# Feature map folded into the query and key weights: six heads per matmul in 120 rows instead of two row tiles of three heads

## The chip, the cores and the metric

The kernel runs on one core of one Trainium2 chip. The metric is the device time of one execution in microseconds (us); lower is better. The time of a kernel is the median of its runs.

## The reference

The kernel computes a linear-attention block with a learned feature map, gated by an MLP. Only block A is touched by the change; what matters of it is:

```
xn   = layernorm(x)                                   # x: 2048 tokens, 640 wide
q, k, v = split(xn @ wqkv)                            # 32 heads of 20 columns each
pq   = einsum("bhsd,hdf->bhsf", q, w_phi)             # one 20x20 matrix per head
pk   = einsum("bhsd,hdf->bhsf", k, w_phi)
phi  = concat(softmax(p), softmax(-p))                # for pq and for pk
o    = phi_q (phi_k^T v) / (phi_q sum(phi_k) + 1e-6)
out  = x + (o @ wo) * silu(gelu(xn @ w1 + b1) @ w2 + b2)
```

Since pq = xn @ (wq of head h @ w_phi of head h), the kernel multiplies the weights with the feature map first and never forms q or k. This product of weights is called the fold here. There are two of them, for keys and for queries, each a 640x640 matrix made from 32 products of 640x20 with 20x20.

## The kernel before, in words

**Stages.** The first stage (to about 259 us of the span) goes over 16 tiles of 128 tokens: each is normalised, transposed on TensorE (`transpose_x`, L293, for the first tiles; the later ones are loaded transposed), and projected (`project`, L307) onto the folded key weights `wk_s`, the value weights `wv_s` and the folded query weights `wq_s`. Feature maps are exponentials per head; `kv_acc` (L378) accumulates phi_k^T v. The second stage is the MLP (L617, L646), the last one the query side and the output projection (L736 to L811). TensorE works in fp32r, with operands split in a high and a low part, in the projections, and in plain fp32 in the fold.

**Where the fold stands.** A fold covers one chunk of 128 input rows (c = 0 to 4) of the key or query weights: `fold(tl, c)` issues its matmuls into one tile `pA` of two PSUM banks, and `fold_w` lets ScalarE copy the result to the high part (L173, fp32r) and VectorE subtract to get the low part (L174). The five key folds come first in the program: folds 0 and 1, the transposes of tile 0, folds 2, 3 and 4, and then the key projection of tile 0. The five query folds stand one by one among the projections of tiles 3 to 6. Tile `pA` has three buffers, which projections, folds and transposes take in turn.

**The operands.** The weights of a fold arrive transposed: in `folds`, partition r and slot i of chunk c hold one column of wq or wk over 128 input rows. Before the change, slot i of six holds heads 3i to 3i+2 of the first 16 heads in partitions 0 to 59, and the same three of the last 16 heads in partitions 64 to 123; slot 5 holds one head of each half, in 20 partitions. `foldb` holds the feature maps of these heads as blocks on a diagonal, 64 columns wide per slot. For each slot two matmuls are issued, one for partitions 0 and up, one for partitions 64 and up, each into its own bank. `_layout`, on the host, only places the inputs in that order.

**What sets the order.** The order on every engine in this part of the program is written out by hand (`manual_schedule`). All loads go through one queue, SP's. It starts with the feature maps (L443), chunk 0 of the key weights (L153), the first tile of x (L131), the other four chunks of the key weights, and two more tiles of x; the five value weights (`raw`, L144), further tiles and the query weights follow. Before the first fold TensorE runs eleven matmuls of a 128x128 tile of ones (L440), which compute nothing that is used.

The rest that the prediction touches: `norm` (L187 to L198 on VectorE, L190 on GpSimd) normalises the next tile; `plain` (L227 on ScalarE, L229 on VectorE) splits a transposed tile; `split_w` (L136, L138) splits the value weights.

Of the kernel before, what the change touches and what calls it, by code (L numbers as in the profile page):

```python
# [8 lines left out]
F32 = mybir.dt.float32  # L9
# [5 lines left out]
S, D, H, DH, F = 2048, 640, 32, 20, 1536  # L15
P = 128
# [4 lines left out]
KC = D // P  # L21
# [24 lines left out]
def hedgehog_gated_mlp_kernel(ctx: ExitStack, tc: tile.TileContext, x, xt_in, wqk, bd, wv, wo, w1, b1, w2, b2, out_t):  # L46
    nc = tc.nc
# [7 lines left out]
    xpool = xstack.enter_context(tc.tile_pool(name="xpool", bufs=1))  # L55
    xpool.tile([P, 16], F32, name="xpad")
    xp = xpool.tile([P, 8, 2, CW], F32R, name="xp")
    foldt = xpool.tile([P, 2 * KC * 6 * P + 6 * 64], F32, tag="D", name="folds")
    folds = foldt[:, :2 * KC * 6 * P].rearrange("p (w c i t) -> p w c i t", w=2, c=KC, i=6)
    foldb = foldt[:, 2 * KC * 6 * P:].rearrange("p (i t) -> p i t", i=6)  # L60
    xds = []
# [21 lines left out]
    def bankA():  # L83
        return pools["A"].tile([P, 2, 512], F32, tag="A", name="pA")
# [73 lines left out]
    def fold(tl, c):  # L158
        ps = bankA()
        for i in range(6):  # L160
            n = 60 if i < 5 else 20
            for hf in range(2):
                r = slice(64 * hf, 64 * hf + n)
                mm = nc.tensor.matmul(ps[:, hf, 60 * i:60 * i + n], tl[r, c, i, :], foldb[r, i, :n],  # L164
                                      start=True, stop=True)
        return ps, mm

    def fold_w(tl, cs, name, dst):
        for c in cs:
            ps, mm = fold(tl, c)  # L170
            sl = slab(F32R, f"{name}{c}")
            s3 = sl[:].rearrange("p s (a b) -> p s a b", a=2)
            nc.scalar.activation(s3[:, 0], ps[:, :, :HALF], AF.Copy)  # L173
            lo = nc.vector.tensor_tensor(s3[:, 1], ps[:, :, :HALF], s3[:, 0].bitcast(F32), op=OP.subtract)  # L174
            dst.append(sl)
        return mm, lo
# [657 lines left out]
    for unit in range(units):  # L834
        h, g = divmod(unit, NG)
# [169 lines left out]
def _layout(A_x, A_wqkv, A_w_phi, A_wo, B_w1, B_b1, B_w2, B_b2):  # L1005
    import numpy as np
    a = {k: np.asarray(v) for k, v in dict(x=A_x, wqkv=A_wqkv, wphi=A_w_phi, wo=A_wo, w1=B_w1, b1=B_b1,
                                           w2=B_w2, b2=B_b2).items()}
    wqk = np.zeros((2, KC, P, FOLD_W), a["wqkv"].dtype)
    bd = np.zeros((P, 6, 64), a["wphi"].dtype)  # L1010
    wo = np.zeros((680, D), a["wo"].dtype)
    for k in range(10):
        wo[64 * k:64 * k + 60] = a["wo"][60 * k:60 * k + 60]
    wo[640:] = a["wo"][600:]
    for h in range(H):
        i, k = divmod(h % 16, 3)
        r = slice(64 * (h // 16) + DH * k, 64 * (h // 16) + DH * (k + 1))
        for w in range(2):
            for c in range(KC):
                wqk[w, c, r, i * P:(i + 1) * P] = a["wqkv"][c * P:(c + 1) * P, w * D + h * DH:w * D + (h + 1) * DH].T  # L1020
        bd[r, i, DH * k:DH * (k + 1)] = a["wphi"][h]
    return [
        ("x", a["x"].reshape(S, D)),
        ("xt", np.ascontiguousarray(a["x"].reshape(S, D).T)),
        ("wqk", wqk),
        ("bd", bd),
        ("wv", np.ascontiguousarray(a["wqkv"][:, 2 * D:])),
        ("wo", wo),
        ("w1", np.ascontiguousarray(a["w1"].reshape(KC, P, NF, P).transpose(2, 1, 0, 3).reshape(NF, P, D))),
        ("b1", np.ascontiguousarray(a["b1"].reshape(NF, P).T)),  # L1030
        ("w2", np.ascontiguousarray(a["w2"])),
        ("b2", np.ascontiguousarray(a["b2"].reshape(KC, P).T)),
    ]
# [18 lines left out]
```

## Time and profile before

| what | value |
|---|---|
| time, median of 3 runs | 693.31 us |
| lowest and highest run | 691.02 and 696.13 us |
| span of the profiled execution | 688.8 us |
| own time of the profiled execution | not shown; the span lies 4.5 us under the median of the runs |
| PE busy | 680.1 us, 99% of the span, 4833 matmul records |
| PEld (weight loads) busy | 592.8 us, 86% |
| VectorE, ScalarE, GpSimd busy | 66%, 36%, 55% |
| mean granted TensorE clock | 0.996 |
| HBM traffic | 125.57 MB, mean 182 GB/s |

The profile shows one execution. PE is TensorE's matmul side and PEld its weight loads; an fp32 matmul of the program leaves two matmul records and two weight loads in the trace, an fp32r matmul one of each. A record's duration holds the pipeline's latency, so the pace of a stream is read from the starts of successive records. A timeline row gives the start, the time from the first start to the last end, the engine, line and operation, the tiles, the shapes (the weights first, then output or moving shape) and the count. Times in rows are us from the span's start.

### The profile page before, as it was taken

To read this page: it belongs to the slowest core of one execution; us is meant where nothing else is said; L and a number is where in the kernel's file an instruction comes from. 1 tells how busy PE (TensorE), PEld (TensorE's weight loads), DVE (VectorE), ACT (ScalarE), POOL (GpSimd) and SP (SyncE) were. 2 spreads that over 40 slices of the span, in tenths; PEclk is the share of its full clock that TensorE was granted. 3 is DMA by queue.
4 is the path that set the end of the run, shared out by engine and by line. 5 is a ranking of instruction groups with operands and counts; after the bars stand their busy time and mean duration, and the time that the engine had idled before them with its cause. 6 is when DMAs were issued, how large, how long until landed. Compare 5 with 4: busy or idle time off the path is not lost.

```text
span 688.8 us, 12182 instructions
## 1 busy us (share of the span) xinstructions
PE 680.1 (99%) x4833; PEld 592.8 (86%) x4833; DVE 453.4 (66%) x730; ACT 251.3 (36%) x398; POOL 376.8 (55%) x336
## 2 busy tenths in 40 slices
PE   8899999999999999999999999999999999999997
PEld 8899999999999998888888888888888887777875
DVE  4688556887667546667978774677977655774232
ACT  3331322332332227343353346632232353425430
POOL 1354344948587455946878853636356640783221
PEclk9999999999999999999999999999999999999999
DMA  9830052824172144328697697276364391886633
GB/s 327 288 104 2 3 149 79 245 68 160 35 212 77 72 145 169 115 69 292 220 328 253 202 429 323 81 272 230 140 218 152 132 391 65 320 292 203 234 92 107
DMA packets 73967, 125.57 MB, mean 182 GB/s; under 512 B 5694, under 2 KB 42686, under 8 KB 73014
## 3 DMA queue, kind: packets, MB, share of 16 engines
q1 hardware_dynamic: 71606, 114.31, 48.8%
q10 hardware_dynamic: 2304, 10.49, 4.3%
q8 instruction: 38, 0.62, 0.4%
q14 instruction: 19, 0.16, 0.1%
HBM read 79.68 MB, written 45.10 MB: 181 GB/s over the span
## 4 chain that ended last, share of the span: by engine, by line
PE 96%; DMA 1%; DVE 1%; issue 1%; POOL 1%; ACT 0%; SPq 0%; POOLq 0%; DVEq 0%
PE pA L307 30%; PE pB L646 24%; PE pB L617 21%; PE pB L805 11%; PE pB L747 3%; PE pA L164 2%; PE pB L736 2%; PE kv L378 2%; DMA folds<-in_wqk_dram 1%; PE pA L293 1%; PE pB L754 1%; PE pB L591 0%; POOL e L328 0%; POOL wv L138 0%; ACT e L333 0%
## 5 line engine op out<-in xcount | busy, mean ns | idle before, releaser
L646 PE MATMUL pB<-hs,w2s 128*128 128x512 f32 x720 | 167.1, 390 | 0.0
L646 PEld LDWEIGHTS pB<-hs,w2s 128*128 128x128 f32 x720 | 134.7, 188 | 29.3 <-PE pB L747 0.8
L617 PE MATMUL pB<-xp,w1s 128*128 128x512 f32 x324 | 81.3, 389 | 0.0
L617 PE MATMUL pB<-xd,w1s 128*128 128x512 f32 x324 | 79.3, 389 | 0.0
L333 ACT ACTIVATE e<-e 128x1280 f32<-128x1280 f32 x32 | 40.7, 1271 | 90.0 <-POOL e L328 90.0
L805 PE MATMUL pB<-oT,wo 128*128 128x512 f32 x300 | 72.9, 395 | 0.0
L655 DVE TENSOR_TENSOR y<-pB,y 128x512 f32<-128x512 f32 x100 | 63.8, 680 | 12.3 <-PE pB L646 12.1
L617 PEld LDWEIGHTS pB<-xd,w1s 128*128 128x128 f32 x324 | 60.8, 188 | 12.6
L617 PEld LDWEIGHTS pB<-xp,w1s 128*128 128x128 f32 x324 | 60.8, 188 | 12.6
L805 PEld LDWEIGHTS pB<-oT,wo 128*128 128x128 f32 x300 | 55.4, 188 | 14.8 <-ACT ph L739 1.2
L346 POOL TENSOR_TENSOR e<-e,rc 128x1280 f32<-128x1280 f32 x16 | 39.0, 2438 | 49.1 <-DVE rc L366 48.8
L346 POOL TENSOR_TENSOR eq<-eq,rc 128x1280 f32<-128x1280 f32 x16 | 37.9, 2370 | 50.2 <-DVE rc L705 50.2
L328 POOL TENSOR_TENSOR e<-nr,e 128x640 f32<-128x640 f32 x32 | 45.5, 1422 | 34.6 <-DVE nr L327 31.7
L307 PE MATMUL pA<-wv,xp 128*128 128x320 f32 x384 | 61.1, 312 | 0.8 <-DVE nr L327 0.4
L307 PE MATMUL pA<-wk,xp 128*128 128x320 f32 x384 | 61.5, 316 | 0.0
L622 ACT ACTIVATE pB<-pB,b1t 128x512 f32<-128x512 f32 x48 | 31.8, 662 | 76.2 <-PE pB L617 26.7
L307 PE MATMUL pA<-wq,xp 128*128 128x320 f32 x384 | 59.0, 309 | 0.0
L307 PEld LDWEIGHTS pA<-wk,xp 128*128 128x128 f32 x384 | 58.3, 193 | 0.2
L307 PEld LDWEIGHTS pA<-wv,xp 128*128 128x128 f32 x384 | 56.9, 188 | 1.7 <-issue 0.7
L307 PEld LDWEIGHTS pA<-wq,xp 128*128 128x128 f32 x384 | 56.9, 188 | 0.1
L692 POOL TENSOR_TENSOR ez<-eq,zrep 128x1280 f32<-128x1280 f32 x16 | 47.3, 2958 | 0.5 <-DMA eq<-e_dram 0.5
L402 POOL TENSOR_TENSOR w1s<-raw,w1s 128x640 fp32r<-128x640 f32 (+1 forms) x18 | 25.7, 1429 | 37.1 <-ACT w1s L401 29.9
(139 smaller groups left out, 1045.2 us busy)
## 6 DMA issues: line engine op xcount, KB each, us to landing
raw<-in_w_dram SPq DMA_DIRECT2D x42, 320.0 KB, 4.4
e_dram<-e ACTq DMA_DIRECT2D x16, 640.0 KB, 4.0
eq<-e_dram SPq DMA_DIRECT2D x16, 640.0 KB, 7.0
phi_dram<-eq SPq DMA_DIRECT2D x16, 640.0 KB, 3.5
phi<-phi_dram SPq DMA_DIRECT2D x16, 640.0 KB, 8.5
xt<-in_x_dram SPq DMA_DIRECT2D x16, 320.0 KB, 4.9
xres<-in_xt_dram SPq DMA_DIRECT2D x20, 256.0 KB, 4.8
out_dram<-xres SPq DMA_DIRECT2D x18, 256.0 KB, 3.0
```

The lines of the kernel that those rows point to most:

```text
L307: nc.tensor.matmul(ps[:, hf, :HALF], stat_x(q, o, k, a), ws[k][:, b, hf * HALF:(hf + 1) * HALF], start=n == 0, stop=n == 3 * KC - 1)
L328: nc.gpsimd.tensor_tensor(e5[:, :, :, 1, :], nr[:, :, :, None].to_broadcast([P, 2, 16, DH]), e5[:, :, :, 0, :], op=OP.subtract)
L333: nc.scalar.activation(ef, ef, AF.Exp)
L346: nc.gpsimd.tensor_tensor(e3, e3, rc[:, :, None].to_broadcast([P, 64, DH]), op=OP.mult)
L402: nc.gpsimd.tensor_tensor(sl[:, 1, :n], src, sl[:, 0, :n].bitcast(F32), op=OP.subtract)
L617: nc.tensor.matmul(bank[ch][:], tl[:, a, off + wo_:off + wo_ + P], mov(blk, b), start=new and n == 0, stop=n == len(mms) - 1, skip_group_c ...
L622: nc.scalar.activation(ps, ps, AF.Gelu_apprx_tanh, bias=b1t[:, f:f + 1])
L646: nc.tensor.matmul(ps[:], ws[i][:, b, d * P:(d + 1) * P], hs[o][i][:, a, :], start=i == n == 0, stop=(i, n) == (GF - 1, 2), skip_group_che ...
L655: nc.vector.tensor_tensor(y, ps[:], y, op=OP.add)
L692: nc.gpsimd.tensor_tensor(zv, ef, zf, op=OP.mult)
L747: nc.tensor.matmul(po[64 * e:64 * e + 64, :256], bdk[:n, 2 * j + e, :], ph[:n, e * 256:(e + 1) * 256], start=True, stop=True)
L805: nc.tensor.matmul(ps[:], w, o, start=n == 0, stop=n == 15)
```

## The change

The six slots of a chunk are filled in another way: slots 0 to 2 hold the first 16 heads (six, six and four of them), slots 3 to 5 the last 16, all from partition 0 on, in 120, 120 and 80 partitions. A fold is then six matmuls of 120 (or 80) rows and 120 (or 80) columns instead of twelve of 60 (or 20). The same columns of the same banks are written. `foldb` becomes 120 columns wide per slot, so its load grows from 384 to 720 values per partition. Nothing else differs: the weights' load has the same size, and all other engines issue the same instructions in the same order. From L164 on, line numbers are lower by one in the changed kernel.

```
-    foldt = xpool.tile([P, 2 * KC * 6 * P + 6 * 64], F32, tag="D", name="folds")
+    foldt = xpool.tile([P, 2 * KC * 6 * P + 6 * 120], F32, tag="D", name="folds")
...
     def fold(tl, c):
         ps = bankA()
         for i in range(6):
-            n = 60 if i < 5 else 20
-            for hf in range(2):
-                r = slice(64 * hf, 64 * hf + n)
-                mm = nc.tensor.matmul(ps[:, hf, 60 * i:60 * i + n], tl[r, c, i, :], foldb[r, i, :n],
-                                      start=True, stop=True)
+            hf, j = divmod(i, 3)
+            n = 120 if j < 2 else 80
+            mm = nc.tensor.matmul(ps[:, hf, 120 * j:120 * j + n], tl[:n, c, i, :], foldb[:n, i, :n],
+                                  start=True, stop=True)
         return ps, mm
...
-    bd = np.zeros((P, 6, 64), a["wphi"].dtype)
+    bd = np.zeros((P, 6, 120), a["wphi"].dtype)
...
-        i, k = divmod(h % 16, 3)
-        r = slice(64 * (h // 16) + DH * k, 64 * (h // 16) + DH * (k + 1))
+        j, k = divmod(h % 16, 6)
+        i, r = 3 * (h // 16) + j, slice(DH * k, DH * (k + 1))
```

The PE queue around a query fold that follows `kv_acc`, in tile 5, before (a row is a run of matmuls: line, operation, output tile and operand, output shape, count):

```order
L378 MATMUL kv<-e,v 32x40 x32
L164 MATMUL pA<-folds 128x60 x10
L164 MATMUL pA<-folds 128x20 x2
L307 MATMUL pA<-wv,b_749 128x320 x12
L307 MATMUL pA<-wv,xp 128x320 x6
```

and the same place in the changed kernel:

```order
L377 MATMUL kv<-e,v 32x40 x32
L163 MATMUL pA<-folds 128x120 x2
L163 MATMUL pA<-folds 128x80
L163 MATMUL pA<-folds 128x120 x2
L163 MATMUL pA<-folds 128x80
L306 MATMUL pA<-wv,b_719 128x320 x12
L306 MATMUL pA<-wv,xp 128x320 x6
```

Twelve matmuls have become six in the same place; the instructions around them stand as before.

The head of SP's queue of loads, before:

```order
L443 DMA folds<-in_bd_dram 128x384
L153 DMA folds<-in_wqk_dram 128x768
L131 DMA xt<-in_x_dram 128x640
L153 DMA folds<-in_wqk_dram 128x768 x4
L131 DMA xt<-in_x_dram 128x640 x2
```

and in the changed kernel:

```order
L442 DMA folds<-in_bd_dram 128x720
L153 DMA folds<-in_wqk_dram 128x768
L131 DMA xt<-in_x_dram 128x640
L153 DMA folds<-in_wqk_dram 128x768 x4
L131 DMA xt<-in_x_dram 128x640 x2
```

The first load is larger; the order is the same.

## The prediction

> **What bounds the kernel now.** First the page's busy shares and its chain that ended last, then TensorE's waits: which engine carries the span, and whether anything holds it up.
>
> ```profile
> PE 96%; DMA 1%; DVE 1%; issue 1%; POOL 1%; ACT 0%; SPq 0%; POOLq 0%; DVEq 0%
> PE pA L307 30%; PE pB L646 24%; PE pB L617 21%; PE pB L805 11%; PE pB L747 3%; PE pA L164 2%; PE pB L736 2%; PE kv L378 2%; DMA folds<-in_wqk_dram 1%; PE pA L293 1%; PE pB L754 1%; PE pB L591 0%; POOL e L328 0%; POOL wv L138 0%; ACT e L333 0%
> PE pA L293 <- DVE xt L198: 1.3, 1, 1.3
> PE pA L440 <- POOL ones L102: 1.2, 1, 1.2
> PE pA L164 <- DMA folds<-in_wqk_dram: 0.5, 1, 0.5
> PE pA L307 <- DVE nr L327: 0.4, 1, 0.4
> PE pA L307 <- POOL wv L138: 0.2, 1, 0.2
> ```
>
> PE carries the chain, and these five are all of its waits, each once and all at the start. So what the fold (L164, 2% of the chain) saves on PE shortens the span, and the most that could be saved is those 2%, some 16 us. The question is the pace of a fold. Here is TensorE's timeline at the start, and the stretch of L440's stream of 128x128 fp32 matmuls with its group's durations (minimum/median/maximum).
>
> ```profile
> 5.49 1.66 PE L164 MATMUL pA<-folds 60*128 60x60 f32 x24
> 7.63 1.66 PE L164 MATMUL pA<-folds 60*128 60x60 f32 x24 [0.48 <-DMA folds<-in_wqk_dram]
> 9.38 0.74 PE L293 MATMUL pA<-ident,xt 128*128 128x128 f32 x5
> 10.05 4.83 PE L164 MATMUL pA<-folds 60*128 60x60 f32 x72
> 14.82 4.44 PE L307 MATMUL pA<-wk,xp 128*128 128x320 f32 x18
> 19.09 0.71 PE L293 MATMUL pA<-ident,xt 128*128 128x128 f32 x5
> 4.83 0.72 PE L440 MATMUL pA<-ones 128*128 128x128 f32 x5
> L440 PE MATMUL pA<-ones x22: 274/421/579, 1.2 to 5.3; 128*128 128x128 f32 x22
> 59.44 1.21 PE L164 MATMUL pA<-folds 60*128 60x60 f32 x17
> ```
>
> The last row is the inside of one query fold. Its 17 records start in nine groups, the odd one and then eight pairs: one row tile of 60 starts together with the other. The eight steps take 1.21 less a last record's 0.272, or 0.94 us: 0.117 us a pair, the first step the longest. In L440 five records take 0.72 us; less the last one's 0.274, four steps of 0.111 us. **So a pair of 60-row records and one full 128x128 record cost the same 0.11 us**: the two tiles already run at once. Three folds in a row take 14.82 - 10.05 = 4.77 us, 1.59 each, for twelve pair steps (1.33 us at 0.111). The 0.26 us beyond them is what a fold loses at its changes of shape, from 128 rows to 60, to 20 and back.
>
> The clock is the second thing in that stretch: the table of stretches, with PE busy, its records, and the granted clock.
>
> ```profile
> 4.00:8.08 4.08, 3.60 (x43) 3.31 (x44) 1.25 (x4) 0.70 (x1) 0.05 (x1) 1.00 0.97 312
> 8.08:11.49 3.41, 3.32 (x49) 2.94 (x47) 2.76 (x4) 1.41 (x2) 0.51 (x1) 1.00 1.03 407
> 11.49:14.90 3.41, 3.41 (x53) 3.19 (x52) 2.21 (x6) 1.41 (x2) 0.28 (x1) 1.00 1.04 410
> 14.90:18.31 3.41, 3.41 (x13) 3.41 (x14) 2.08 (x3) 0.70 (x1) 0.27 (x1) 0.50 1.03 408
> ```
>
> For 3.41 us right behind the key folds the clock is halved, though PE was busy for all 3.41 us before. What was low there is how much the matmuls feed: a fold streams ten pair steps of 60 columns and two of 20, 640 columns in 1.59 us, while L440's pace would bring 128 x 1.59/0.111 = 1830; that is 35%.
>
> **The change, part by part.** *Query folds.* Each becomes 12 records, six of 120 (or 80) columns twice, one after the other. Three of the five stand between projections. The rows of such a place, and of the same projections without a fold:
>
> ```profile
> 36.85 2.00 PE L307 MATMUL pA<-wv,xp 128*128 128x320 f32 x12
> 38.70 4.56 PE L307 MATMUL pA<-wk,xp 128*128 128x320 f32 x30
> 43.19 0.84 PE L378 MATMUL kv<-e,v 128*32 128x40 f32 x64
> 43.96 2.91 PE L307 MATMUL pA<-wv,xp 128*128 128x320 f32 x18
> 46.71 0.71 PE L293 MATMUL pA<-ident,xt 128*128 128x128 f32 x5
> 57.49 2.00 PE L307 MATMUL pA<-wv,xp 128*128 128x320 f32 x12
> 59.43 1.66 PE L164 MATMUL pA<-folds 60*128 60x60 f32 x24
> 61.02 4.66 PE L307 MATMUL pA<-wk,xp 128*128 128x320 f32 x30
> 65.61 0.84 PE L378 MATMUL kv<-e,v 128*32 128x40 f32 x64
> 78.48 1.66 PE L164 MATMUL pA<-folds 60*128 60x60 f32 x24
> 80.07 2.03 PE L307 MATMUL pA<-wv,b 128*128 128x320 f32 x12
> ```
>
> With the fold 61.02 - 57.49 = 3.53 us, without it 38.70 - 36.85 = 1.85: 1.68. The projection behind takes 65.61 - 61.02 = 4.59 against 43.19 - 38.70 = 4.49, so 0.10 more, its first weight load being late. That is 1.78 us a fold. Now 12 x 0.111 = 1.33 in unbroken 128-row work: a gain of 0.45, three times 1.35. The other two follow `kv_acc`, whose own tiling spoils the next load anyway: 80.07 - 78.48 = 1.59 becomes 1.33, twice 0.26. Together **-1.87 us**.
>
> The step of 0.111 us has bounds. The trace holds no 120-row fp32 stream of 120 columns. If columns set the pace, the step shrinks to 0.111 x 120/128 = 0.104 and 0.111 x 80/128 = 0.069: a fold of 1.11, another 0.22 less. If the weight load is no longer hidden, the 0.10 of the late load comes on each record: 0.21. I take 0.111, since 60 columns and 128 have the same step, which speaks for the weight load, 128 columns in both, as what sets it; and L440, one full tile behind the other, is the nearest row.
>
> *The larger first load.* 128 x 336 x 4 bytes = 172 kB at 312 to 410 GB/s is 0.42 to 0.55 us; I take 0.45, as the next loads run near 407. All loads behind it land that much later. Fold 0 is covered: it starts 0.2 us after the last L440 and shows no wait. Fold 1 isn't, its chunk ends its wait now: 7.63 becomes 8.08, and the transposes of tile 0, whose load shifts as well, 9.83 for 9.38.
>
> *Key folds.* The rows of VectorE that the next steps lean on:
>
> ```profile
> 9.15 1.75 DVE L174 TENSOR_TENSOR wk<-pA,wk 128x640 fp32r<-128x640 f32 x2
> 12.49 0.82 DVE L174 TENSOR_TENSOR wk<-pA,wk 128x640 fp32r<-128x640 f32 x1 [0.77 <-ACT wk L173]
> 15.21 0.61 DVE L198 TENSOR_SCALAR xt<-xt,st 128x640 f32<-128x640 f32 x1 [0.67 <-POOL st L190]
> 15.74 1.55 DVE L174 TENSOR_TENSOR wk<-pA,wk 128x640 fp32r<-128x640 f32 x2
> 20.64 0.42 DVE L229 TENSOR_TENSOR b<-pA,b 128x256 fp32r<-128x256 f32 x1 [3.35 <-ACT xp L227]
> ```
>
> Fold 2 takes fold 0's buffer, free halfway through the 9.15 row at 10.0; now 10.5. Three folds of 1.33 end at 14.5 for 14.82: **-0.30 us**, the late load paid. Cover for the rest: fold 3's buffer must be free for tile 1's transposes, and the tile normalised; VectorE does this by 16.5 (half of the 15.74 row) plus 0.45, so 17.0.
>
> *The clock.* A fold now streams 8 x 120 + 4 x 80 = 1280 columns in 1.33 us, 83% of L440's pace. So I expect the halved stretch to go. The first 18 matmuls of the key projection take 19.09 - 14.82 = 4.27 us now, and 46.71 - 43.96 = 2.75 elsewhere at the full clock (likewise with a late first load): **-1.52 us**. By the clock itself, 3.41 x 0.5 = 1.71; I keep the rows. Tile 1's transposes then start at 14.5 + 2.75 = 17.25, just behind the 17.0 of VectorE, and for 19.09. From there a chain over VectorE, GpSimd and ScalarE leads to the value projection at 33; it starts with ScalarE's copy of these transposes and VectorE's L229 (20.64), and moves with them. From 33 on PE is dense, and nothing is seen to wait, so I let the whole shift stand.
>
> The sum is -1.87 - 0.30 - 1.52 = -3.7 us. Against its own execution: a span of 688.8 becomes 685.1. Its own time isn't shown; its span lies 4.5 us under the median of 693.31. With that kept, **689.6 us**.
>
> **What the Trainium skill says.** "TensorE: Matmul & The Clock Gate", section "HAM oscillation — how this bites in real kernels", has it that the clock falls where PE idles for more than about 3.4 us between bursts. The trace differs: PE was busy for all of the 3.41 us before the fall. By that rule the fold's shape would not matter to the clock, which is the first rival below. The same page of the Trainium skill, in the section "The mechanism" of its Part 3, says that weight loads overlap with matmuls in flight only when their row groups differ, as they did between the two row tiles and no longer do. L440's 0.111 us speaks against it; by that rule the second rival would come.
>
> **The rivals.** (1) *The clock falls all the same* (it hangs on something else than columns streamed). For it: I have one fall in one execution, and the stretch 8.08 to 11.49, also thin in columns, was not followed by one. Against: nothing else is special there. Then only -1.87 - 0.30 = -2.2: 691.1 us. (2) *Slower: each weight load waits for the matmul before it*, in the fold's own stream. Before, successive loads went to different row tiles. At 0.21 us a record a fold takes 2.53 us: query folds 3 x (2.53 - 1.78) + 2 x (2.53 - 1.59) = +4.1; fold 1 from 8.08 to 10.6, the transposes to 11.3, three folds to 18.9, +4.1 for 14.82, and the clock's fall stays. 701.5 us. It decides from 0.13 us a record on (2.2 us over 120 records is 0.018 above 0.111). Against it stands L440's pace on full rows. (3) *The later first load thins out the start*: fold 0 ends near 6.9, fold 1 waits to 8.08, and the idle gap brings a fall of the clock from there, 1.7 us on the folds, in place of the one lost: about -3.7 + 1.7, 691.3 us. For it: a wait of 1.1 us instead of 0.48. Against: fold 0 alone streams 1280 columns there instead of 640.
>
> **How the numbers follow.** The forecast 0.60, the first rival 0.23, the third 0.11, the second 0.06. All but one lie within 1% (6.9 us), which is about what a measurement of this kernel can tell from no change. The three runs of before lie 5.1 us apart, so a median can be off by 2 us or more. The range goes from 686.5 (the forecast, less the 2.2 of the column-paced step and some scatter) to 694.0 (rivals 1 and 3 with the scatter of runs); only rival 2 is left out. Faster by over 1% needs the column-paced step and luck in the runs, 0.07; slower by over 1% is rival 2, 0.06; the rest 0.87.
>
> **What would show it.** L164's work becomes 120 records at line 163, with steps of 0.11 us and no gap inside; a query fold between projections adds 1.33 us. No stretch of half clock behind the key folds, and tile 1's transposes at about 17.3 us. Fold 1 begins near 8.1. Steps of 0.2 us would prove the sum wrong, and so would a new wait on PE past 33 us that eats the shift, or a clock that still falls.

## The result and the profile after

| | before | changed |
|---|---|---|
| median of the runs, us | 693.38 (6 runs) | 687.54 (6 runs) |
| lowest to highest | 691.02 to 696.13 | 687.44 to 688.63 |
| span of the profiled execution | 688.8 | 686.9 |
| mean granted clock in it | 0.996 | 0.999 |

The time ratio is 0.9896, with a 95% interval from 0.9867 to 0.9924: about 1% faster, or 7.2 us of 693.4 by the ratio and 5.8 by the medians. The forecast was 3.7. The two profiled spans differ by only 1.9 us, and the runs of before are spread over 5 us, those of the changed kernel over 1.2. Both have to be explained.

First the folds themselves. The changed kernel's timeline of PE at the start:

```profile
6.06 1.60 PE L163 MATMUL pA<-folds 120*128 120x120 f32 x12
8.66 1.56 PE L163 MATMUL pA<-folds 120*128 120x120 f32 x12 [0.99 <-DMA folds<-in_wqk_dram]
10.39 0.74 PE L292 MATMUL pA<-ident,xt 128*128 128x128 f32 x5 [0.17 <-DVE xt L197]
11.03 4.25 PE L163 MATMUL pA<-folds 120*128 120x120 f32 x36
15.07 2.89 PE L306 MATMUL pA<-wk,xp 128*128 128x320 f32 x18
17.79 0.71 PE L292 MATMUL pA<-ident,xt 128*128 128x128 f32 x5
```

and its query folds, with the same projections without one:

```profile
37.40 4.56 PE L306 MATMUL pA<-wk,xp 128*128 128x320 f32 x30
41.89 0.84 PE L377 MATMUL kv<-e,v 128*32 128x40 f32 x64
45.87 2.00 PE L306 MATMUL pA<-wv,xp 128*128 128x320 f32 x12
47.72 1.92 PE L306 MATMUL pA<-wk,b 128*128 128x320 f32 x12
56.19 2.00 PE L306 MATMUL pA<-wv,xp 128*128 128x320 f32 x12
58.04 1.46 PE L163 MATMUL pA<-folds 120*128 120x120 f32 x12
59.30 4.64 PE L306 MATMUL pA<-wk,xp 128*128 128x320 f32 x30
63.86 0.84 PE L377 MATMUL kv<-e,v 128*32 128x40 f32 x64
76.28 1.57 PE L163 MATMUL pA<-folds 120*128 120x120 f32 x12
77.65 2.00 PE L306 MATMUL pA<-wv,b 128*128 128x320 f32 x12
```

By the same subtraction as in the prediction: 59.30 - 56.19 = 3.11 less 47.72 - 45.87 = 1.85 is 1.26 us, and the projection behind it takes 63.86 - 59.30 = 4.56 against 4.49. So a fold between projections costs 1.33 us for 1.78, and one behind `kv_acc` 77.65 - 76.28 = 1.37 for 1.59. Three at 0.45 and two at 0.22 are 1.8 us. The three key folds in a row take 15.07 - 11.03 = 4.04 us, 1.35 each, for 1.59.

Then the clock: the changed kernel's table of stretches (length, busy time and records of PE, PEld, VectorE, ScalarE, GpSimd, then the granted clock).

```profile
6.34:9.75 3.41, 2.42 (x21) 2.27 (x21) 1.37 (x5) 0.70 (x1) 0.56 (x1) 1.00 1.01 397
9.75:13.16 3.41, 3.25 (x29) 2.98 (x28) 2.88 (x4) 1.94 (x3) 0.00 (x0) 1.00 1.03 409
13.16:16.57 3.41, 3.41 (x29) 3.41 (x29) 2.46 (x6) 1.58 (x3) 0.56 (x1) 1.00 1.05 416
16.57:19.99 3.42, 3.42 (x27) 3.41 (x26) 2.25 (x5) 1.45 (x4) 0.00 (x0) 1.00 1.02 407
```

No stretch is at half clock, even where PE was busy for only 2.42 of 3.41 us. This execution is the slowest of the six, at 688.63 us: there PE waits once in the MLP, a wait that the profile of before does not have. The wait, the addition on VectorE ahead of it, and the same addition in before:

```profile
PE pB L616 <- DVE pB L888: 1.0, 1, 1.0
361.71 3.45 DVE L670 TENSOR_TENSOR xhi<-xhi,xlo 128x1280 f32<-128x1280 f32 x1
364.17 2.68 DVE L671 TENSOR_TENSOR xhi<-xhi,xlo 128x1280 f32<-128x1280 f32 x1
```

VectorE comes late there. The addition took 3.45 us for 2.68, and two rows ahead of it took longer as well: L698 1.59 us (1.18 before) and L704 0.87 (0.59). The addition alone doesn't make the wait: a later profile of the changed kernel (span 684.7 us) has it at 3.44 us, L698 at 0.72, and no wait. Why these rows differ between executions isn't known. The changed kernel's lead at the start of the MLP is 258.6 - 255.4 = 3.2 us; the wait takes about 1 us of it, and 1.9 are left at the end.

### The profile page after: what moved, and what is told of

It reads as the page before. It is cut to its first block, busy times and chain, and to the rows that moved or that the text cites. A ratio compares the mean times of both kernels' runs of the same rounds, so it can differ in the third digit from the quotient of the medians.

```text
span 686.9 us, 11941 instructions
## 1 busy us (share of the span) xinstructions
PE 676.7 (99%) x4713; PEld 590.6 (86%) x4713; DVE 455.5 (66%) x730; ACT 251.3 (37%) x398; POOL 375.6 (55%) x336
## 4 chain that ended last, share of the span: by engine, by line
PE 90%; DVE 5%; ACT 1%; issue 1%; DMA 1%; POOL 1%; SPq 0%; DVEq 0%; POOLq 0%; ACTq 0%
PE pA L306 30%; PE pB L645 22%; PE pB L616 18%; PE pB L804 11%; PE pB L746 3%; PE pB L735 2%; PE kv L377 2%; PE pA L163 2%; DVE y L654 2%; DVE xhi L670 1%; DMA xt<-in_x_dram 1%; PE pA L292 1%; PE pB L753 1%; DVE rc L340 0%; PE pB L590 0%
## 5 line engine op out<-in xcount | busy, mean ns | idle before, releaser
L306 PE MATMUL pA<-wk,xp 128*128 128x320 f32 x384 | 59.9, 311 | 0.0
L306 PEld LDWEIGHTS pA<-wk,xp 128*128 128x128 f32 x384 | 56.8, 188 | 0.1
```

Source lines behind the costliest of these rows:

```text
L306: nc.tensor.matmul(ps[:, hf, :HALF], stat_x(q, o, k, a), ws[k][:, b, hf * HALF:(hf + 1) * HALF], start=n == 0, stop=n == 3 * KC - 1)
```

## The experiments

**What was to be told apart.** A run's time is its span plus 1.7 or 1.8 us in each run for which both are noted (688.63 and 686.9; 692.98 and 691.2). So the profiled execution of before took about 690.5, faster than any of the six runs beside it, and of the 4.5 us between its span and the median, which the prediction kept as they were, 2.8 were something else. Theory A: the clock falls in the key folds of before, in most runs for longer than in the profiled one, because a fold streams few columns per time. Theory B: those runs wait somewhere else. Against the columns stands a rival on the cause of the fall: the form, 60 rows in two row tiles.

**The kernel before, again**, with the clock of each run.

> The kernel before, unchanged, for the span and the granted clock of each of its runs. The runs of before lie 4.5 us above their profiled span, those of the change 0.6 above theirs. Theory A (the clock falls more often or longer in most runs of before than in the one that was profiled): spans from about 688 to 694 us, and the mean clock lower by about 0.0025 for each 1.7 us of span, down to about 0.992. Theory B (a wait outside the folds, in the MLP, comes in some runs): spans differ as much, but the mean clock stays near 0.996 in all of them.

Its 12 runs took 691.69 to 697.31 us, median 696.49, at mean clocks of 0.987 to 0.998; the lowest lie under the 0.992 expected. With the runs of before that were taken beside this and later kernels there are 66 with a noted clock, and the clock orders them:

| mean clock of the run | runs | time, us: median (lowest to highest) |
|---|---|---|
| 0.987 | 10 | 697.4 (696.7 to 698.1) |
| 0.988 to 0.990 | 39 | 696.1 (695.2 to 697.0) |
| 0.992 to 0.995 | 12 | 692.8 (691.8 to 694.3) |
| 0.996, 0.997 | 3 | 690.6 (690.5 to 691.1) |
| 0.998 | 2 | 691.7, 691.9 |

On a straight line fitted through all of them, 0.001 of clock costs 0.62 us. The profile of this kernel's run (691.2 us of span) shows a fall twice as long as in the first profile:

```profile
6.72:13.55 6.83, 6.83 (x101) 6.28 (x99) 4.93 (x10) 2.80 (x4) 0.56 (x1) 1.00 1.03 411
13.55:20.38 6.83, 6.83 (x39) 6.67 (x40) 3.34 (x8) 1.41 (x2) 0.55 (x1) 0.50 1.03 410
20.38:23.80 3.42, 3.42 (x27) 3.41 (x26) 1.37 (x4) 2.16 (x5) 0.00 (x0) 1.00 1.01 389
```

PE is busy for all of the 6.83 us ahead of the fall. Theory A holds in that the times move with the clock, which theory B would have left near 0.996; whether it is the columns that move the clock is for the next kernels to show. The two runs at 0.998 are slower than the line says; what they lost otherwise isn't known.

**Row tiles, but 120 columns each.** The upper columns of the feature map are zeros, and the next matmul overwrites what they write.

```
-    foldt = ... + 6 * 64], ...
+    foldt = ... + 6 * 120], ...
-                mm = nc.tensor.matmul(ps[:, hf, 60 * i:60 * i + n], tl[r, c, i, :], foldb[r, i, :n],
+                mm = nc.tensor.matmul(ps[:, hf, 60 * i:60 * i + 120], tl[r, c, i, :], foldb[r, i, :],
-    bd = np.zeros((P, 6, 64), a["wphi"].dtype)
+    bd = np.zeros((P, 6, 120), a["wphi"].dtype)
```

> Row tiles and twelve matmuls as before, but each streams 120 columns, of which the upper part is zeros that the next matmul overwrites; the first load is as large as in the change. Theory A by columns (the clock falls because a fold streams few columns): steps stay at 0.11 us a pair, the fall of the clock behind the key folds is gone, and the time is 1.5 to 5 us below before, 688.5 to 692. Rival by form (the clock falls because only 60 rows or two row tiles work at once): the fall stays, and the time is before's, 693 to 694.

Median 690.90 us (690.43 to 691.48, 7 runs), ratio 0.9942 (0.9919 to 0.9964), all clocks 0.998 or higher. Its timeline at the start:

```profile
5.98 1.79 PE L164 MATMUL pA<-folds 60*128 60x120 f32 x24
8.41 1.79 PE L164 MATMUL pA<-folds 60*128 60x120 f32 x24 [0.64 <-DMA folds<-in_wqk_dram]
10.21 0.74 PE L293 MATMUL pA<-ident,xt 128*128 128x128 f32 x5
10.88 5.24 PE L164 MATMUL pA<-folds 60*128 60x120 f32 x72
16.05 2.90 PE L307 MATMUL pA<-wk,xp 128*128 128x320 f32 x18
18.79 0.71 PE L293 MATMUL pA<-ident,xt 128*128 128x128 f32 x5
```

Three folds take 16.05 - 10.88 = 5.17 us, longer than before's 4.77 (the last slot streams 120 columns too); yet the projection behind takes 18.79 - 16.05 = 2.74 us, at the full clock, and the kernel is faster, though PE's added work is of no use. The rival by form falls: the row tiles are all still there, and no run has a clock under 0.998.

**Only the key folds, only the query folds.** Each side's slots are laid out in the old or the new way, with a feature map of its own; the second is loaded ahead of the query weights.

```
+        if tl is folds_new[0]:
+            for i in range(6):
+                hf, j = divmod(i, 3)
+                n = 120 if j < 2 else 80
+                mm = nc.tensor.matmul(ps[:, hf, 120 * j:120 * j + n], tl[:n, c, i, :], foldn[:n, i, :n], ...)
+            return ps, mm
```

> Only the key folds have six heads per matmul; the query folds keep the row tiles, with a load of their own for the feature maps. Theory A: all of the clock's part and 0.3 us of shapes, so 1.8 us by the profile and up to 4.5 by the runs: 689 to 691.5. Theory B: 0.3 to 1.8 us: 691.5 to 693.

> Only the query folds have six heads per matmul. Both theories: 1.8 us less from pace and shapes, 691.5; the fall of the clock behind the key folds stays, and under theory A so do runs some us apart.

Keys alone: 688.73 us (688.08 to 690.28, 6 runs), ratio 0.9910 (0.9881 to 0.9938), all clocks 0.999 or higher. That is a little under the range expected, which was counted from a before of 693.4; before, beside it, was at 696.08. Queries alone: 692.95 us (686.94 to 696.06, 12 runs), ratio 0.9964 (0.9937 to 0.9990), clocks from 0.986 to 0.999, all but one at 0.997 or lower; 691.5 was expected, from the same 693.4. The key folds carry the falls; the query folds, 1.6 us each between dense projections, cause none, since none is left in the keys-only kernel. The profile of the queries-only kernel shows how long a fall can be (its three folds in a row, the projection behind them, then its stretches):

```profile
11.33 8.67 PE L174 MATMUL pA<-folds 60*128 60x60 f32 x72
19.93 5.17 PE L317 MATMUL pA<-wk,xp 128*128 128x320 f32 x18
5.27:8.68 3.41, 2.96 (x43) 2.67 (x44) 1.99 (x6) 0.70 (x1) 0.56 (x1) 1.00 0.96 360
8.68:12.09 3.41, 3.41 (x27) 2.92 (x25) 1.43 (x2) 1.35 (x2) 0.00 (x0) 0.50 1.03 409
12.09:25.75 13.66, 13.66 (x91) 13.15 (x89) 4.97 (x9) 2.16 (x4) 0.55 (x1) 0.50 0.88 350
25.75:29.16 3.41, 3.41 (x25) 3.41 (x25) 2.05 (x6) 2.64 (x5) 0.03 (x1) 1.00 0.39 99
```

It begins inside fold 1 and lasts 12.09 - 8.68 + 13.66 = 17.07 us, five times 3.41; this execution took 695.67 us. One run of this same kernel, at 0.999, took 686.94. Between them lie 8.7 us in one kernel.

**Full rows, but half the columns at a time.** The reverse of the wide row tiles.

```
+            m = n // 2
+            for o in (0, m):
-                mm = nc.tensor.matmul(ps[:, hf, 120 * j:120 * j + n], tl[:n, c, i, :], foldb[:n, i, :n],
+                mm = nc.tensor.matmul(ps[:, hf, 120 * j + o:120 * j + o + m], tl[:n, c, i, :], foldb[:n, i, o:o + m],
```

> The change with each matmul cut in two halves of its columns: full rows, no row tiles, but 60 (or 40) columns to each weight load, so a fold is 24 records one after the other, some 2.66 us, and streams about 42% of the full pace. Columns theory: the clock falls in most runs, as before, mean clocks 0.985 to 0.996, and the time is the change's 687.5 plus 13.3 us for the records plus 2 to 6 for the falls, 703 to 707. Form theory: no falls, clocks 0.998 and up, 701.

Median 704.82 us (703.70 to 705.15, 4 runs), ratio 1.0131 (1.0088 to 1.0175), clocks 0.993, 0.989, 0.989, 0.989. The fall is back without any row tile (folds 0 and 1, the transposes behind them, then the stretches around the fall):

```profile
5.30 5.45 PE L165 MATMUL pA<-folds 120*128 120x60 f32 x48
10.58 0.74 PE L294 MATMUL pA<-ident,xt 128*128 128x128 f32 x5
11.30:14.71 3.41, 3.41 (x34) 3.41 (x32) 1.56 (x3) 1.49 (x3) 0.00 (x0) 1.00 1.04 410
14.71:28.37 13.66, 13.66 (x62) 13.62 (x61) 4.24 (x8) 1.41 (x2) 0.55 (x1) 0.50 0.65 260
28.37:31.78 3.41, 3.41 (x26) 3.41 (x25) 1.94 (x6) 2.64 (x5) 0.00 (x0) 1.00 0.38 99
```

Folds 0 and 1 take 10.58 - 5.30 = 5.28 us for 48 records, 0.11 each: a record of 60 or 40 columns is no shorter than one of 120. In the last stretch before the fall PE and PEld are both busy for all of it. With the wide row tiles this shows the cause by both edits: columns streamed per time, not row tiles or idle gaps, and zeros count as columns too. What stays untested is the rows: nearly every step of these kernels has 120 rows at work, in one tile or in two, so a clock that follows rows times columns would do the same.

The profiles allow a closer count. The granted clock changes at the edges of stretches of 3.41 us, which lie at other places of the program in each execution (at 4.66 us in the first profile of before, at 6.72 and 5.27 in the two others with row tiles and a fall). Counting the columns of the matmuls that start in each stretch at full clock, a pair once, against L440's pace, the four stretches ahead of a fall hold 34%, 37%, 41% and 43%, and all others in the first 35 us of the 14 profiles 42% or more. A few per cent of the records can be missing, so this is a bound near 42%, not a sharp one. It would also explain why one kernel shows falls of so different lengths: it depends on where an edge meets the folds.

**No matmul of 20 rows; 90 columns in row tiles.** Two points between.

```
-            n = 60 if i < 5 else 20
+            n = 60
```

> The kernel before with its last slot filled up with zeros to 60 rows and 60 columns, so that no matmul of 20 rows stands in a fold and the array changes its shape once less each way; 47% of the full pace in columns. If the lost 0.26 us of a fold sits at the change from 60 rows to 20 and back, the last records' gap of 0.2 us is gone and a fold lasts about 0.1 us less; the falls of the clock, by the columns theory, come less often than before or shorter, if the bound lies near half, and as before if it lies higher.

```
-                mm = nc.tensor.matmul(ps[:, hf, 60 * i:60 * i + 120], tl[r, c, i, :], foldb[r, i, :],
+                mm = nc.tensor.matmul(ps[:, hf, 60 * i:60 * i + 90], tl[r, c, i, :], foldb[r, i, :90],
```

> As the run with 120 columns in row tiles, but with 90 columns: some 60% of the full pace. Columns theory: where the bound lies under 60%, no falls and about 690 us as with 120; where it lies higher, falls as before and 693 to 696.

The first: median 694.48 us, ratio 0.9958 (0.9921 to 0.9994); its ten runs lie in two heaps, four at 687.48 to 688.41 with clocks 0.999 and up, six at 694.43 to 697.26 with 0.987 to 0.989. Its four fast runs are about as fast as the changed kernel. The second: 690.26 us (689.47 to 690.74, 6 runs), ratio 0.9922 (0.9895 to 0.9949), no fall. Three folds of the first, profiled in a run without a fall, then one of its query folds, then three folds of the second:

```profile
9.89 4.23 PE L164 MATMUL pA<-folds 60*128 60x60 f32 x72
14.05 2.91 PE L307 MATMUL pA<-wk,xp 128*128 128x320 f32 x18
57.13 1.55 PE L164 MATMUL pA<-folds 60*128 60x60 f32 x24
58.62 4.66 PE L307 MATMUL pA<-wk,xp 128*128 128x320 f32 x30
9.72 5.08 PE L164 MATMUL pA<-folds 60*128 60x90 f32 x72
14.74 2.90 PE L307 MATMUL pA<-wk,xp 128*128 128x320 f32 x18
```

The first's folds take (14.05 - 9.89)/3 = 1.39 us for 720 columns, 45% of L440's pace (the 47% expected counts the steps alone); the second's (14.74 - 9.72)/3 = 1.67 us for 1080 columns, 56% and not 60%. Together with before (35%, two of 66 runs at 0.998, all others lower) and the half columns (42%, falls in four runs of four), the bound for a whole fold lies at 45% or a little above, and under 56%. The time lost at the 20 rows is confirmed as well: three folds in a row take 1.39 us each and not 1.59, twice the gain expected; a lone query fold takes 58.62 - 57.13 = 1.49, as expected.

**The first loads.** Tile 0 of x ahead of the feature maps; the feature maps in 20 columns per slot, spread by VectorE with a mask; both; and the change itself beside them.

```
-    nc.sync.dma_start(foldb, bd)
-    wkT = load_fold(1, lambda: x_in(0))
+    x_in(0)
+    nc.sync.dma_start(foldb, bd)
+    wkT = load_fold(1)
```

> The change, with tile 0 of x loaded first, ahead of the feature maps. In the profile of the change the transposes of tile 0 wait for that tile's chain and start at 10.4 us. If the first loads set the start, the transposes follow fold 1 at once and everything behind is 0.3 to 0.7 us earlier: 687.0. If chunk 1 of the weights, whose landing stays where it is, sets it alone, the same as the change.

```
-    nc.sync.dma_start(foldb, bd)
+    nc.sync.dma_start(foldc, bd)
+    nc.vector.tensor_tensor(foldb[:120].rearrange("p i (k d) -> p i k d", d=DH),
+                            foldc[:120, :, None, :].to_broadcast([120, 6, 6, DH]),
+                            xpad[:120, None, :6, None].to_broadcast([120, 6, 6, DH]), op=OP.mult)
```

> The change, unchanged, on one chip with the next three. Columns theory: every mean clock 0.998 or higher, 687 to 689 us, whatever the runs of before do beside it.

> The change with the feature maps loaded in 20 columns to a slot (120 values per partition instead of 720) and spread over the diagonal by one VectorE multiplication with a mask. If the larger first load costs the start its time (the query folds alone gave 686.9 in a run without a fall), all loads land 0.7 us earlier and the time is 0.5 to 0.9 us less than the change's. If the start hangs on something else, the same.

> Both, tile 0 of x first and the small load. If the two gains add up, 1.3 to 1.9 us under the change, 685.5 to 686.2; if both lift the same wait, as the better of the two alone.

> Tile 0 of x first, with the full load, again, beside the change on the same chip. If the first look was right, 0.7 to 1.2 us under the change in this call.

| kernel | median of 6 runs, us (lowest to highest) | measured |
|---|---|---|
| x first | 686.52 (686.02 to 686.99) | earlier, without the change beside it |
| the change again | 686.64 (686.46 to 688.17) | together with the next three |
| small load | 686.17 (685.78 to 686.70) | together |
| x first and small load | 686.28 (685.53 to 686.96) | together |
| x first, again | 686.98 (686.67 to 687.49) | together |

The gain of x first, expected at 0.7 to 1.2 us, isn't there beside the change itself. The small load is 0.5 us lower, with ranges that overlap; whether it is faster stays open. The two together are no faster than the small load alone. The change repeated its ratio, 0.9890 (0.9860 to 0.9919), all six clocks 0.998 or higher, at a median a little under the 687 to 689 expected. A run of it was profiled at a span of 684.7 us, without the wait in the MLP.

## Why the prediction was right or wrong, point by point

**The pace of a fold** was right. The step of a record was forecast at 0.111 us; twelve records at 1.33 us are what the rows give, and the five query folds gained 1.8 us for 1.87. The shorter step, paced by columns, on which the range's lower end rested, did not come. The rival in which each weight load waits for the matmul before it is out: full-row loads, one behind the other, were hidden. That differs from what the Trainium skill says in "TensorE: Matmul & The Clock Gate", Part 3, "The mechanism": there a load overlaps with a matmul in flight only in another row group. The same section of the Trainium skill also lets a load into the background weight buffer run ahead of matmuls in flight, and that would allow what was seen.

**The cause of the clock's fall** was right, and the cure. Columns per time decide, with the reservation on rows above; the changed kernel has no run under 0.998 in twelve, and the rival that the clock falls all the same is out. So is the rival of a fall through the idle gap: the change waits 0.99 us ahead of fold 1, and the clock stays. The Trainium skill's rule in "TensorE: Matmul & The Clock Gate", section "HAM oscillation — how this bites in real kernels", is about idle gaps of more than some 3.4 us; in three of the four profiles with a fall PE was busy for all of the 3.41 us ahead of it, and in the fourth for 2.96, so the rule does not cover this case.

**The size of the clock's term failed.** The prediction put it as 19.09 - 14.82 = 4.27 against 2.75, "-1.52 us", one fall of 3.41 us at the end of the folds. For the profiled pair that is right: the changed kernel takes 17.79 - 15.07 = 2.72 us there, 1.55 less. But that was one of the mildest executions. In 49 of 66 runs of before the mean clock is 0.990 or lower; a fall of 6.83 us was profiled in before, and one of 17.07 in the queries-only kernel, whose key folds are the same. An early fall also feeds itself: at half clock the three folds last 19.93 - 11.33 = 8.6 us for 4.77, so that their columns come more slowly still, and in all four profiles with a fall the clock came back only after the projection had begun.

What the falls cost in a median run can be worked out from the kernels that have none, by taking back what their folds gain or lose on their own. Keys alone, 688.73, plus the 0.7 us of three shorter folds gives 689.5 for before without falls; 120 columns in row tiles, 690.90, less 1.05 for its longer folds, 689.9; 90 columns, 690.26, less 0.65, 689.6. So falls took some 3.5 to 4 us of the first median of 693.38, and some 6.5 of the 696.08 beside the experiments, where 1.5 were forecast. The two runs of before at a clock of 0.998, at 691.7 and 691.9, don't fit by 2 us, and the queries-only kernel's one run without a fall, 686.94 plus the query folds' 1.8, gives 688.7; the cost is settled to some 2 us, not better.

**The step from the span to the median failed with it.** "With that kept": the 4.5 us between 688.8 and 693.31 were kept as a fixed cost. Fixed are 1.7. The other 2.8 were, by the table of clocks, mostly longer falls (the clocks of those first runs themselves weren't noted), and the change takes them away. Had they been read so, 3.7 + 2.8 = 6.5 us would have been the forecast, and 5.8 to 7.2 came.

**The key folds' 0.30 and the first load's 0.45** can't be seen in the runs. In the profiles the three folds are 0.73 us shorter, but starts differ by more from one execution to the next: the transposes of tile 0, forecast at 9.83 us, began at 10.39 in the change's first profile and at 9.36 in the repeated one, of the same kernel, and the three folds ended at 15.07 and 14.05, for 14.82 in before and 14.5 forecast. The small load's 0.5 us is at the edge of what the runs tell.

**That nothing waits past 33 us** held in the repeated profile and not in the first one, where the MLP's wait took about 1 us.

## What to carry to other kernels

Before a gap between a profiled span and the median of the runs is called overhead, compare the two for the same execution: here 2.8 of 4.5 us were not overhead but most likely the clock, and the spread of the runs was the clue. A stream of matmuls with few columns to each 128-column weight load can keep PE busy and still lose it the clock, for several times 3.41 us; look for it where a startup or a small matrix product runs for more than a few microseconds. Putting more rows and columns into each matmul cost no time per step here. It did not save steps either: two row tiles already ran at once, so a fold stayed at twelve steps, and what was gained was the changes of shape and the clock. Where the rows are given, columns of zeros held the clock and gained 0.6 and 0.8%.

## What the runs showed of the hardware

- The granted clock fell to 0.50 behind folds at 35% and 42% of the column pace of 128x128 fp32 matmuls, in three of four profiles with PE busy for all of the 3.41 us ahead; at 45% six of ten runs had a mean clock of 0.989 or lower. In the 55 runs of kernels whose key folds stream 56% or more, the mean clock was 0.998 or higher, and none of the profiles shows a fall.
- Falls lasted 3.41, 6.83, 13.66 and 17.07 us: whole multiples of 3.41.
- A pair of matmuls in two row tiles of 60 rows (0.117 us a step with 60 columns) costs as much as one of 120 rows (0.11): the row tiles ran at once, and gained nothing over full rows. Records of 120 rows with 60 or 40 columns took 0.11 us as well.
- A change from 60-row to 20-row tiles and back cost 0.2 us a fold in three folds in a row (1.59 against 1.39), and 0.1 in a lone one (1.59 against 1.49).
